# Window attention and a SwiGLU feed-forward on one core: one PSUM pool, RMS chains for pairs of blocks, the attention steps placed by hand, and two more blocks transposed by DMA

## The chip, the cores and the metric

One core of a Trainium2 chip. The metric is the time of one execution of the kernel in microseconds (us), on the device. The profile's span (first to last instruction) is 1.7 to 2.4 us shorter than that time.

Names: PE is TensorE, DVE is VectorE, ACT is ScalarE, POOL is GpSimd, SP is SyncE. "L393" is line 393 of that kernel's source.

## The reference, cut to what matters

```python
def reference(q, k, v, n_sink=4, window=128, w_gate, w_val, w_out, rms_g):
    # q, k, v: 4 batches x 8 heads x 768 positions x 64
    scores = q @ k.T / 8          # kept: the 4 first keys ("sink"), and the last 128 keys
    a = softmax(where(keep, scores, -1e9))
    x = heads side by side (a @ v)               # 3072 tokens x 512
    xn = x / sqrt(mean(x*x) + 1e-6) * rms_g
    g = xn @ w_gate;  val = xn @ w_val           # 512 x 1536 each
    return (g * sigmoid(g) * val) @ w_out        # 1536 x 512
```

## The kernel before

The 3072 tokens are 24 blocks of 128 (six blocks a batch: 0 to 5, 6 to 11, 12 to 17, 18 to 23). Four blocks make a group of the feed-forward part (FFN), so there are six groups, G0 to G5. FFN matmuls of group G are cut into "parts" (four matmuls of 512 columns, 0.86 us of PE by the trace: one part starts at 76.43 us in the kernel before, the next at 77.29), and the attention of later blocks is woven between the parts. A block's "chain" is the row of small DVE instructions that makes 1/sqrt of its mean square (RMS); `xr` is the attention's output times that, and `x(g)` brings it transposed to the FFN as `xnt`. `t(g)` transposes q and k of a block (`qkT`), by a DMA where `by_dma(g)` is true and else on PE (`DMA_T_FROM` is 12, `NT` is 6), `s(g)` makes its scores. `FA` is how many of G0's 12 FFN tiles are done in two halves, first for blocks 0 and 1, later for blocks 2 and 3. PE's and SP's orders are the program's; the order of DVE, ACT and POOL is chosen by the compiler's scheduler, except in the prologue.

```python
def by_dma(g):                      # who transposes q and k of block g: a DMA, or PE
    return g >= DMA_T_FROM and g % NT > 0        # DMA_T_FROM = 12, NT = 6

def unit_sink(b):                   # once a batch: the four sink keys, repacked
    ks = sink.tile([P, HP * KSW], BF16, name="ksk")
    nc.vector.memset(ks, 0.0)
    ksv = ks.rearrange("p (h c) -> p h c", c=KSW)
    for hi in range(2):
        pr = slice(hi * D, (hi + 1) * D)
        nc.vector.tensor_copy(out=ksv[pr, :, hi * NS:(hi + 1) * NS],
                              in_=QKT[b][pr, 1, :, 0:NS])   # keys of the batch's FIRST block
    ...                             # cut

def val():                          # in an FFN part; gate() has made th = tanh(pg / 2)
    pvl = mms("pvl", wv, G, fts, cols)           # a PSUM bank
    nc.vector.scalar_tensor_tensor(out=p1, in0=th, scalar=1.0, in1=pg, ...)   # reads PSUM
    nc.vector.tensor_tensor(out=HT[key], in0=p1, in1=pvl, ...)  # reads PSUM, frees the bank

def step(g):                        # what of the attention goes with block g
    ...                             # cut: sink scores, scores of g, attention of g-1
    if t == 1:
        slots[1].append(lambda: unit_sink(b))    # one step after the batch's first block
    if g + 2 < NB and not by_dma(g + 2):
        slots[2 if t != 5 else 1].append(lambda: unit_t(g + 2))
    if g + 3 < NB and by_dma(g + 3):
        slots[2].append(lambda: unit_t(g + 3))
    ...                             # cut
```

Two things matter later. First, `unit_sink(2)` reads the transposed keys of block 12, and `unit_sink(3)` those of block 18. The condition `g % NT > 0` keeps just these blocks on PE. Second, by the program a PSUM bank that holds `pg` or `pvl` is used again only when DVE has done its product, and the banks are taken in turn.

The softmax here doesn't subtract the row's maximum and nothing guards it: scores larger than these inputs give would overflow.

Of the kernel before, what the change touches and what calls it, by code (L numbers as in the profile page):

```python
# [28 lines left out]
def kernel(  # L29
# [26 lines left out]
    GB = 4  # L56
    NG = NB // GB
    GN = GB * P
# [8 lines left out]

    DMA_X_FROM = 8
    FA = 10
    WEAVE_FROM = 9  # L70
    POOL_MASK_FROM = 2
# [4 lines left out]
    ld = ctx.enter_context(tc.tile_pool(name="ld", bufs=3 * NT))  # L76
# [10 lines left out]
    pools = ExitStack()  # L87
    pp = [pools.enter_context(
        tc.tile_pool(name="psum0", bufs=2, space=bass.MemoryType.PSUM)
    )]  # L90
    PROLOGUE = [True]
    WARM = (3, 4, 5, 2)
# [6 lines left out]
    gb = const.tile([P, DM], FP32, name="gb")  # L99

# [21 lines left out]
    def load_v(g):  # L122
        b, t = divmod(g, NT)
        nc.gpsimd.dma_start(  # L124
            out=V16[b][:, t, :, 0:D],
            in_=v[b, :, t * P:(t + 1) * P, :].rearrange("h t d -> t h d"),
        )

# [30 lines left out]
    raw = [opool.tile([P, DM], FP32, name="osb") for _ in range(3)]  # L159
    for i, src in enumerate((q, k)):  # L160
# [4 lines left out]
    nc.sync.dma_start(  # L165
        out=raw[2][0:1, :], in_=moe_rms_g.rearrange("(o d) -> o d", o=1),
    )
    nc.vector.memset(gb[0:1, 0:P], 1.0)

# [4 lines left out]

    def unit_gb():
        ps = pp[0].tile([P, 512], FP32, name="pgb", tag="ph", bufs=6)
        nc.tensor.matmul(
            out=ps, lhsT=gb[0:1, 0:P], rhs=raw[2][0:1, :], start=True, stop=True,
        )
        nc.scalar.copy(out=gb, in_=ps)  # L180

    with tc.manual_schedule(engines={mybir.EngineType.Pool, mybir.EngineType.DVE}):
# [16 lines left out]
        unit_cast(1)  # L199
        load_k(1)  # L200
# [21 lines left out]
        for g in range(GB + 1, 2 * GB):  # L222
            load_q(g)
            load_k(g)
            load_v(g)
        load_wo(0)
        last_load = load_wo(1)
    with tc.issue_after(last_load):
        for g in range(2 * GB, NB):
            load_q(g)  # L230
            load_k(g)
            load_v(g)


# [9 lines left out]
    def unit_t1(g, i):  # L244

        b, t = divmod(g, NT)
        if t == 0 and i == 0:
            QKT[b] = qkt.tile([P, 2, HP, S], BF16, name="qkT")
        kind = dict(tag="ph", bufs=6) if PROLOGUE[0] and g == 2 else dict(tag="b1")
        ps = pp[0].tile([P, 512], FP32, name="pqk", **kind).bitcast(BF16)  # L250
        transposes(ps, (QS, KS_)[i].pop(g), 0)
        (nc.scalar.copy if g != 1 and i == 0 else nc.vector.tensor_copy)(
            out=QKT[b][:, i, :, t * P:(t + 1) * P],
            in_=ps[:, 0:HP * P].rearrange("p (x c) -> p x c", c=P),
        )

    def by_dma(g):
        return g >= DMA_T_FROM and g % NT > 0

    def unit_t(g):  # L260
# [10 lines left out]
        ps = pp[0].tile([P, 512], FP32, name="pqk", tag="b1").bitcast(BF16)  # L271
# [7 lines left out]
    def unit_sink(b):  # L279
# [11 lines left out]
        for half in range(2):  # L291
            ps = pp[0].tile([P, 512], FP32, name="pvs", tag="b1")
# [14 lines left out]
    def unit_sink_scores(b, t):  # L307

        w = 2 * P
        ps = pp[0].tile([P, 512], FP32, name="pss", tag="b1")  # L310
# [12 lines left out]
    def unit_warm(n):  # L323

        ps = pp[0].tile([P, 512], FP32, name="pw", tag="ph", bufs=6)
# [4 lines left out]

    PTS = {}

    def unit_bias(g, n):

        if PROLOGUE[0]:
            banks = [pp[0].tile([P, 512], FP32, name="ph", tag="ph", bufs=6)
                     for hi in range(2)]
        else:
            banks = [bank() for hi in range(2)]
# [31 lines left out]
    def bank():  # L371
        return pp[0].tile([P, 512], FP32, name="pT", tag="b1")

    def mask(ev, b, t, nq):
        x = ev.shape[1]
        if b < POOL_MASK_FROM or t == 0:
# [16 lines left out]
    def unit_s(g):  # L393
# [17 lines left out]
        for u in range(nb):  # L411
            et = epool.tile([P, 2, per, nq, P], BF16, name="et")
            for hi in range(2):
# [4 lines left out]
                if nq == 1:  # L418
                    mask(et[:, hi], b, t, nq)
            if nq == 2:  # L420
                mask(et.rearrange("p i j n c -> p (i j) n c"), b, t, nq)
            for j in range(per):
                for hi in range(2):
                    for n in range(nq):
                        E[(g, 2 * (u * per + j) + hi, n)] = et[:, hi, j, n, :]

    def halves(g):

        return [slice(0, DM // 2), slice(DM // 2, DM)] if g == 1 else [slice(0, DM)]
# [3 lines left out]
    def unit_sink_av(g):  # L433
        b, t = divmod(g, NT)
        for u in range(2):
            PVB[(g, u)] = pp[0].tile([P, 512], FP32, name="pv", tag="b1")
# [8 lines left out]
    def unit_av(g, u):  # L445
        b, t = divmod(g, NT)

        pv = PVB.pop((g, u)) if t >= 2 else pp[0].tile(
# [12 lines left out]
        if u == 0:  # L461
            X16[g] = xpool.tile([P, H, D], BF16, name="x16")
# [3 lines left out]
        else:  # L466
            unit_norm(g, u, pvv)
            unit_sq(g, u)
        if u == 1 and g >= 2:
            unit_rms(g)  # L470
# [19 lines left out]
    def unit_sq(g, u):  # L490
        if u == 0:
            MS[g] = small.tile([P, 2], FP32, name="ms")
# [4 lines left out]
            accum_out=MS[g][:, u:u + 1],  # L497
        )

    def unit_rms(g):  # L500
        x16 = X16.pop(g).rearrange("p h d -> p (h d)")
        ms = MS.pop(g)
        m = small.tile([P, 1], FP32, name="m")
        nc.vector.scalar_tensor_tensor(
            out=m, in0=ms[:, 0:1], scalar=RMS_EPS, in1=ms[:, 1:2],
# [3 lines left out]
        y = small.tile([P, 5], FP32, name="y")  # L509
        nc.vector.tensor_scalar(  # L510
            out=y[:, 0:1].bitcast(I32), in0=m.bitcast(I32), scalar1=-0.5,
            scalar2=float(0x5f3759df - 2 ** 31), op0=ALU.mult, op1=ALU.add,
        )
        nc.vector.scalar_tensor_tensor(
            out=y[:, 1:2], in0=y[:, 0:1], scalar=y[:, 0:1], in1=m,
            op0=ALU.mult, op1=ALU.mult,
        )
        nc.vector.scalar_tensor_tensor(
            out=y[:, 2:3], in0=y[:, 1:2], scalar=RSQRT_B, in1=y[:, 1:2],
# [3 lines left out]
            out=y[:, 3:4], in0=y[:, 1:2], scalar=RSQRT_A, in1=y[:, 0:1],  # L523
# [3 lines left out]
            out=y[:, 4:5], in0=y[:, 2:3], scalar=RSQRT_C, in1=y[:, 3:4],  # L527
            op0=ALU.add, op1=ALU.mult,
        )
        Y[g] = y  # L530
        X16[g] = x16
        if g >= 2:
            unit_xr(g)

    Y = {}

    def unit_xr(g):
        y, x16 = Y.pop(g), X16.pop(g)
        XR[g] = []
        for c in halves(g):  # L540
            XR[g].append(xpool.tile([P, c.stop - c.start], BF16, name="xr", bufs=3))
            nc.vector.scalar_tensor_tensor(  # L542
                out=XR[g][-1], in0=x16[:, c], scalar=y[:, 4:5], in1=gb[:, c],
                op0=ALU.mult, op1=ALU.mult,
            )
        if g >= DMA_X_FROM:
            G, tb = divmod(g, GB)
            if tb == 0:
                XNT[G] = xtpool.tile([P, KTN, GN], BF16, name="xnt")
            nc.sync.dma_start_transpose(  # L550
                out=XNT[G][:, :, tb * P:(tb + 1) * P], in_=XR.pop(g)[0],
            )

    def unit_x(g):
# [3 lines left out]
        if tb == 0:  # L558
            XNT[G] = xtpool.tile([P, KTN, GN], BF16, name="xnt")
        for xr, c in zip(XR.pop(g), halves(g)):  # L560
            n = c.stop - c.start
            ps = pp[0].tile([P, 512], FP32, name="pxt", tag="b1").bitcast(BF16)
            for i in range(n // P):
                nc.tensor.transpose(
                    out=ps[:, i * P:(i + 1) * P], in_=xr[:, i * P:(i + 1) * P],
                    identity=ident,
                )
            nc.scalar.copy(  # L568
                out=XNT[G][:, c.start // P:c.stop // P, tb * P:(tb + 1) * P],
                in_=ps[:, 0:n].rearrange("p (k c) -> p k c", c=P),  # L570
            )
# [4 lines left out]
    def mms(name, w_sb, G, fts, cols):  # L576

        ps = pp[0].tile([P, 512], FP32, name=name, tag="b1")
# [37 lines left out]
    def parts_o(G, tb):  # L616
        st = {}

        def part(i):
            if i == 0:  # L620
                st["po"] = pp[0].tile([P, 512], FP32, name="po", tag="b1")
# [15 lines left out]
    def step(g):  # L637


        b, t = divmod(g, NT)  # L640
        slots = [[], [], [], []]
# [6 lines left out]
        if g <= NB:  # L648
            if (g - 1) % NT >= 2:
                slots[0].append(lambda: unit_sink_av(g - 1))  # L650
            slots[0].append(lambda: unit_av(g - 1, 0))
            slots[0].append(lambda: unit_av(g - 1, 1))
        if GB <= g - 3 < NB:
            slots[1].append(lambda: unit_x(g - 3))
        if g + 2 < NB and not by_dma(g + 2):
            slots[2 if t != 5 else 1].append(lambda: unit_t(g + 2))
        if g + 3 < NB and by_dma(g + 3):
            slots[2].append(lambda: unit_t(g + 3))
        return slots

    def weave(parts, slots, upto=0, first=False):

        n, i = len(parts) - upto, 0
        for s, f in enumerate(parts):
            if first:
                f()
            while i < len(slots) and i < (s + 1) * len(slots) / n:
                for u in slots[i]:
                    u()
                i += 1  # L670
            if not first:
                f()

    with tc.manual_schedule(engines=MANUAL_ALL):
        unit_warm(6)
# [6 lines left out]
        unit_bias(1, 0)  # L682
        unit_sp(0, 1)
        unit_t1(1, 1)
# [7 lines left out]
        unit_warm(WARM[0])  # L692
        for u in range(2):
            unit_av(1, u)
            unit_norm(1, u, PV[(1, u)])
            unit_sq(1, u)
        unit_gb()
        unit_rms(0)
        unit_xr(0)
        unit_rms(1)  # L700
        unit_xr(1)
        unit_warm(WARM[1])
        unit_x(0)
        unit_t1(2, 0)
        unit_warm(WARM[2])
        unit_x(1)
# [4 lines left out]
        pools.close()  # L711
        pp[0] = ctx.enter_context(
            tc.tile_pool(name="psum", bufs=8, space=bass.MemoryType.PSUM)
        )
        PROLOGUE[0] = False

    with tc.manual_schedule(engines=MANUAL):

# [7 lines left out]
        weave(fa, [  # L726
# [64 lines left out]
```

## Time and profile before

255.18 us, median of three runs (254.96 to 256.45).

The page of the kernel before: busy time by engine, then the busy tenths of PE and the granted clock in 40 slices of 6.4 us.

```profile
PE 240.8 (95%) x1784; PEld 125.2 (49%) x1784; DVE 175.7 (69%) x465; ACT 141.9 (56%) x320; POOL 94.8 (37%) x127
...
PE   6988899989979999999999999999999999999994
...
PEclk9979999999999999999999999999999999999999
```

PE is nearly always busy, so what can be won is time in which PE waits or runs at a lower clock, and work that is taken from it. Note the 7 in the third slice of the clock.

To see how much that is I set the columns of all matmuls (512 columns in 213 ns, the trace's own spacing; the two fp32 ones counted double, which is an estimate: the trace of before has 1.06 us for both of them together, 0.53 us each; warm-up matmuls left out) against the time, stage by stage; a stage ends where the next group's first gate matmul starts. "Lost" is time less work. Small negative values come from rounding the spacing.

| stage | before: time | work | lost | after: time | work | lost |
|---|---|---|---|---|---|---|
| prologue | 19.4 | 5.6 | 13.8 | 16.2 | 4.9 | 11.2 |
| G0 | 57.0 | 51.7 | 5.3 | 55.5 | 47.2 | 8.3 |
| G1 | 36.6 | 36.7 | -0.2 | 48.8 | 40.6 | 8.2 |
| G2 | 37.2 | 37.2 | 0.0 | 38.9 | 36.7 | 2.2 |
| G3 | 36.6 | 37.1 | -0.5 | 38.8 | 37.1 | 1.7 |
| G4 | 32.9 | 32.4 | 0.5 | 33.3 | 32.4 | 0.9 |
| G5 and tail | 34.9 | 30.7 | 4.2 | 35.1 | 30.7 | 4.4 |

The end of the prologue before, in order of time (start, duration, engine, line, operation, out<-in; in brackets the idle time ahead of it and what ended it). PE only:

```profile
15.68 0.63 PE L239 MATMUL pqk<-ident,qs 128*128 128x128 bf16 x4
16.10 2.34 PE L327 MATMUL pw<-idle 128*128 128x512 bf16 x5
18.23 0.63 PE L564 MATMUL pxt<-ident,xr 128*128 128x128 bf16 x4
19.39 0.38 PE L582 MATMUL pg<-xnt,wg 128*128 128x256 bf16 x2 [0.52 <-DMA ks<-in_k_dram]
```

Five idle (warm-up) matmuls take 2.34 us, 427 ns apart, twice the 213 ns, and the granted clock is 0.50 from 15.3 to 18.7 us; the transposes of block 1 stand behind them. The first gate matmul is at 19.4.

What DVE waited for, before (sum, times, longest, us), and what the tile `ksk`, the sink keys, waited for in the same kernel:

```profile
DVE p L600 <- ACT th L595: 18.9, 28, 10.3
DVE rden L480 <- PE pv L457: 10.0, 7, 4.3
DVE m L504 <- ACT sq L495: 9.0, 12, 1.6
```

```profile
its engine sat idle before it (us, times) until:
  issue: 3.0, 8
  PE pss L312: 0.4, 1
  ACT qkT L274: 0.2, 1
```

DVE never waits for a DMA in the main part; the copies of the sink keys wait 0.2 us at most for their keys.

### The profile page before, as it was taken

How to read it: one execution, taken by the hardware profiler on the slowest of the kernel's cores; microseconds unless marked ns; L12 is line 12 of the kernel's file. 1: busy time of each engine (PE TensorE's matmuls, PEld its weight loads, DVE VectorE, ACT ScalarE, POOL GpSimd, SP SyncE). 2: the span in 40 equal slices, each digit the busy share in tenths (PEclk: the TensorE clock that was granted, in tenths of full speed). 3: DMA queues.
4: the chain of work that ended last, by engine and by line, in shares of the span. 5: the costliest groups of instructions: out<-in, count | busy, mean ns of one | idle time of the engine just before them, and what ended most of it. 6: DMA issues, size and time to landing. Idle time of an engine off the chain costs nothing.

```text
span 254.6 us, 4880 instructions
## 1 busy us (share of the span) xinstructions
PE 240.8 (95%) x1784; PEld 125.2 (49%) x1784; DVE 175.7 (69%) x465; ACT 141.9 (56%) x320; POOL 94.8 (37%) x127
## 2 busy tenths in 40 slices
PE   6988899989979999999999999999999999999994
PEld 2536677755534444454454444444444444444441
DVE  4563897998768999348898277998268991277800
ACT  2646678879994565475475366566445341333211
POOL 8986778299987440331231003033121000000000
PEclk9979999999999999999999999999999999999999
DMA  9999999999999999435005328215321101200022
GB/s 130 142 171 190 188 157 189 183 156 155 185 174 168 156 155 118 97 89 147 10 12 64 82 62 147 41 23 64 104 61 45 21 18 63 107 0 0 3 82 82
DMA packets 105849, 25.74 MB, mean 101 GB/s; under 512 B 95073, under 2 KB 102753, under 8 KB 105826
## 3 DMA queue, kind: packets, MB, share of 16 engines
q0 software_dynamic: 80704, 13.90, 70.6%
q1 hardware_dynamic: 24082, 11.28, 20.0%
q10 hardware_dynamic: 1040, 0.26, 0.5%
q8 instruction: 14, 0.23, 0.4%
q14 instruction: 9, 0.07, 0.1%
HBM read 28.31 MB, written 6.29 MB: 136 GB/s over the span
## 4 chain that ended last, share of the span: by engine, by line
PE 68%; DVE 12%; ACT 8%; POOL 4%; DMA 3%; issue 2%; POOLq 0%; DVEq 0%; ACTq 0%
PE po L623 20%; PE pg L582 20%; PE pvl L582 19%; DVE hT L608 3%; DVE p L600 3%; DMA ks<-in_k_dram 3%; PE pT L405 2%; ACT et L414 2%; DVE et L380 2%; ACT sq L495 2%; PE pv L453 2%; PE pv L457 2%; ACT qkT L274 1%; DVE x L485 1%; POOL qs L111 1%
## 5 line engine op out<-in xcount | busy, mean ns | idle before, releaser
L582 PE MATMUL pg<-xnt,wg 128*128 128x512 bf16 (+1 forms) x328 | 74.0, 353 | 2.3 <-ACT xnt L568 1.8
L582 PE MATMUL pvl<-xnt,wv 128*128 128x512 bf16 (+1 forms) x328 | 74.0, 353 | 0.0
L595 ACT ACTIVATE th<-pg 128x512 bf16<-128x512 f32 x72 | 43.2, 600 | 51.2 <-PE pg L582 49.8
L623 PE MATMUL po<-wo,hT 128*128 128x512 bf16 x288 | 64.9, 379 | 0.1
L600 DVE SCALAR_TENSOR_TENSOR p<-th,pg 128x512 bf16<-128x512 bf16 x72 | 49.2, 683 | 18.9 <-ACT th L595 18.9
L608 DVE TENSOR_TENSOR hT<-p,pvl 128x512 bf16<-128x512 bf16 x72 | 49.4, 686 | 5.7 <-PE pvl L582 0.9
L582 PEld LDWEIGHTS <-wg 128*128 128x128 bf16 x328 | 31.4, 98 | 30.9 <-issue 2.7
L582 PEld LDWEIGHTS <-wv 128*128 128x128 bf16 x328 | 31.2, 98 | 28.8 <-issue 0.2
L414 ACT ACTIVATE et<-pT 128x512 bf16<-128x512 f32 x76 | 39.5, 605 | 6.7 <-PE pT L405 6.7
L623 PEld LDWEIGHTS <-hT 128*128 128x128 bf16 x288 | 27.4, 98 | 30.6 <-issue 0.2
L382 POOL TENSOR_SCALAR_AFFINE_SELECT et<-et 128x512 bf16<-128x512 bf16 x20 | 12.6, 637 | 79.7 <-ACT et L414 73.2
L630 ACT ACTIVATE osb<-po 128x512 f32<-128x512 f32 x24 | 14.4, 601 | 27.8 <-PE po L623 25.4
L495 ACT ACTIVATE sq<-x 128x256 bf16<-128x256 bf16 x48 | 20.2, 425 | 7.5 <-DVE x L485 7.1
L111 POOL DMA_DIRECT2D qs<-in_q_dram x23 | 20.9, 907 | 7.0 <-DMA wo<-in_moe_w_out_dram 2.5
L111 POOL DMA_DIRECT2D ks<-in_k_dram x23 | 20.8, 904 | 6.6 <-DMA wo<-in_moe_w_out_dram 2.9
L124 POOL DMA_DIRECT2D v<-in_v_dram x24 | 21.7, 903 | 4.3 <-DMA qs<-in_q_dram 2.7
L485 DVE TENSOR_TENSOR x<-pv,rden 128x256 bf16<-128x256 f32 x48 | 20.0, 422 | 0.9
L380 DVE TENSOR_TENSOR et<-et,masks 128x1024 bf16<-128x1024 bf16 (+1 forms) x22 | 13.9, 636 | 8.5 <-ACT et L414 8.4
L542 DVE SCALAR_TENSOR_TENSOR xr<-x,y,gb 128x512 bf16<-128x512 bf16 (+1 forms) x25 | 18.1, 728 | 0.7
L480 DVE RECIPROCAL rden<-pv 128x4 f32<-128x4 f32 x48 | 7.8, 173 | 10.1 <-PE pv L457 10.0
L405 PE MATMUL pT<-qkT 64*128 64x256 bf16 (+1 forms) x168 | 12.0, 261 | 2.1 <-ACT qkT L274 1.4
L457 PE MATMUL pv<-v,et 128*128 128x65 bf16 x168 | 12.6, 194 | 0.0
(72 smaller groups left out, 198.3 us busy)
## 6 DMA issues: line engine op xcount, KB each, us to landing
out_dram<-osb SPq DMA_DIRECT2D x24, 256.0 KB, 2.2
v<-in_v_dram POOLq DMA_DIRECT2D x24, 128.0 KB, 7.6
qs<-in_q_dram POOLq DMA_DIRECT2D x23, 128.0 KB, 7.5
ks<-in_k_dram POOLq DMA_DIRECT2D x23, 128.0 KB, 7.5
wg<-in_moe_w_gate_dram POOLq DMA_DIRECT2D x6, 256.0 KB, 8.6
wv<-in_moe_w_val_dram POOLq DMA_DIRECT2D x6, 256.0 KB, 8.9
wo<-in_moe_w_out_dram POOLq DMA_DIRECT2D x2, 768.0 KB, 10.7
osb<-in_k_dram ACTq DMA_DIRECT2D x1, 256.0 KB, 4.5
```

What stands on the lines that cost most here:

```text
L111: nc.gpsimd.dma_start(out=tl, in_=src[b, :, t * P:(t + 1) * P, :].rearrange("h t d -> t h d"),)
L124: nc.gpsimd.dma_start(out=V16[b][:, t, :, 0:D], in_=v[b, :, t * P:(t + 1) * P, :].rearrange("h t d -> t h d"),)
L380: nc.vector.tensor_tensor(out=e, in0=e, in1=mv, op=ALU.mult)
L414: nc.scalar.activation(out=et[:, hi].rearrange("p j n c -> p (j n c)"), in_=banks[u][hi], func=ACT.Exp, scale=inv_sqrt_d,)
L485: nc.vector.tensor_tensor(out=X16[g][:, heads_of(g, u), :], in0=pvv[:, :, 0:D], in1=RDEN.pop((g, u)).unsqueeze(2).to_broadcast((P, 4, D)), ...
L495: nc.scalar.activation(out=sq, in_=xh, func=ACT.Square, scale=MS_SCALE, accum_out=MS[g][:, u:u + 1],)
L542: nc.vector.scalar_tensor_tensor(out=XR[g][-1], in0=x16[:, c], scalar=y[:, 4:5], in1=gb[:, c], op0=ALU.mult, op1=ALU.mult,)
L582: nc.tensor.matmul(out=ps[:, i * n:(i + 1) * n], lhsT=w_sb[:, kt, ft * P:(ft + 1) * P], rhs=XNT[G][:, kt, cols], start=(kt == 0), stop=(kt ...
L595: nc.scalar.activation(out=st["th"], in_=st["pg"], func=ACT.Tanh, scale=0.5)
L600: nc.vector.scalar_tensor_tensor(out=p1, in0=st["th"], scalar=1.0, in1=st["pg"], op0=ALU.add, op1=ALU.mult,)
L608: nc.vector.tensor_tensor(out=HT[key][:, i:i + n, cols], in0=p1.rearrange("p (n c) -> p n c", n=n), in1=pvl.rearrange("p (n c) -> p n c", ...
L623: nc.tensor.matmul(out=st["po"], lhsT=HT[(G, ft // 2)][:, ft % 2, tb * P:(tb + 1) * P], rhs=wo[:, ft, :], start=(ft == 0), stop=(ft == FTN ...
```

## The change

Its intent, as its text shows: shorten the prologue (one RMS chain for blocks 0 and 1, the RMS weight multiplied in while their transposes are copied out of PSUM, more warm-up matmuls), use one PSUM pool of eight banks throughout, halve the number of small RMS instructions on DVE by doing two blocks in one chain, put DVE's masks and chains some parts later (`later`), give every attention unit a part number by hand, and take the transposes of blocks 12 and 18 from PE too. The core of the diff:

```diff
-    FA = 10
+    FA = 8                                   # FFN tiles of G0 that are done in two halves
 ...
     def by_dma(g):
-        return g >= DMA_T_FROM and g % NT > 0
+        return g >= DMA_T_FROM
 ...
-        if u == 1 and g >= 2:
-            unit_rms(g)
+        if u == 1 and g >= 2 and g % 2 == 1:
+            later(0 if g < GB else 1 if g < 2 * GB else 3, lambda: unit_rms(g))
 ...                                          # cut: unit_rms works on [P, 2] instead of [P, 1]
+        for i in range(2):
+            later(0 if g < GB else 1 if g < 2 * GB else 1 + i, lambda i=i: unit_xr(g - 1 + i, y[:, 5, i:i + 1]))
 ...                                          # cut: unit_x multiplies by gt at evacuation, ACT and DVE share it
-        if g + 3 < NB and by_dma(g + 3):
-            slots[2].append(lambda: unit_t(g + 3))
+            slots[2].append(lambda: unit_t(g + 2))
+        if g + 4 < NB and by_dma(g + 4):
+            slots[2].append(lambda: unit_t(g + 4))
 ...
-        unit_warm(6)
+        unit_warm(9)
 ...                                          # cut: prologue order; 28 warm-ups instead of 18
+        run(fb[:8], [
+            (0, lambda: unit_bias(3, 1)),
+            (0, lambda: unit_sp(3, 1)),
+            (0, lambda: unit_x(2)),
+            (0, lambda: unit_x(3)),
 ...                                          # cut: part numbers of all other units of G0
+                for g in range(8 if G == 1 else 4 * G + 6, min(4 * G + 10, NB + 1)):
+                    p = 6 * (g - 8) if G == 1 else 9 * (g - 4 * G - 6)
+                    slots += step(g, p, 1.5 if G == 1 else 2)
```

## The prediction

> **What bounds the kernel now.** TensorE. The share table has PE busy 95%, and the windows view has it at 10.0 of 10 us from 80 us on at full clock. All matmuls' columns at the trace's own rate (512 in about 213 ns) make 231 us without the 18 warm-ups; the span is 254.6. So 24 us are lost:
> - Prologue: the first gate matmul starts at 19.4 us (timeline), after about 5 us of real matmul work: 14.5 lost.
> - 19 to 80 us: about 5 us net, in gaps between matmul starts: 0.9 at 22.7 (ACT qkT copy), 0.9 at 26.7 (DVE qkT copy), 0.7 at 37 (xnt of blocks 2, 3), 0.7 at 49, 1.1 at 53 (qkT), 0.5 at 65, 1.7 at 74.6 (xnt of block 7, right before the next group's gate).
> - Tail: about 4 us of last eviction and store.
>
> **What the change does.**
> 1. Prologue. Before, the block-1 RMS chain starts only at 15.14, behind xr(0), which waited for the copy of gb (0.57 us on ACT); its xr takes two STT pieces of 0.48 us on DVE; then its transposes wait behind five warm-up matmuls that ran at clock 0.5 (15.3 to 18.7, windows view: 427 ns each), start at 18.23, and the two ACT copies end at 19.34. After: one chain for both blocks from about 14.0, seven small ops, about 1.2 us; xr(0) as tensor_scalar on DVE at about 0.3 us (the same kind on 512 bf16 elements, the mask conversion, took 0.29; the STT takes 0.75), xr(1) at once on ACT, about 0.6; evictions split over ACT and DVE, 1 to 1.2 us for both. First gate at about 17.2: 2.2 us earlier. [...] 28 warm-ups instead of 18, 12 in that gap, should keep the clock whole.
> 2. Blocks 12 and 18 are transposed by DMA: 16 matmuls of 128 columns fewer, about 0.85 us of PE, where PE is the bound: all gained.
> 3. Placement by hand in parts (masks, squares and chains put off, x(6), x(7) a part earlier): of the 4.5 us lost between 40 and 80 I expect 2 to 3 back. But pairing means that x(2), x(3) wait for block 3's chain right before the second half of group 0: norms, squares, 1.2 us chain, evictions with gt (four small ACT muls or one 0.7 us DVE op), against 4 us of PE work in between: a wait of 1 to 2 us near 30 us. It eats much of the 2.5 us saved in that stage.
> 4. 12 pair chains for 24 save about 10 us of DVE, off the critical path.
>
> **Sum:** -2.2 - 0.85 - 2.4 = about -5.5 us: 249.7.
>
> **Prediction:** 249.7 us, 247.0 to 252.8 in 8 of 10. Chances: faster by over 2% 0.53, within 2% 0.44, slower 0.03.
>
> **What would show it:** first pg at 17 to 17.5; clock 1.0 between 15 and 19; one wait of 1 to 2 us for xnt of blocks 2 and 3; none over 0.5 us at the turn from group 0 to 1; PE gapless after 80; 16 fewer PE transposes.
>
> **What would make it wrong:** the 12 warm-ups running at half clock and pushing x(0) back; the gt load of 4-byte pieces holding up others; DVE near full (about 85% by my count) while group 1 carries five blocks' attention, so that PSUM banks come free late; DMA transposes of the x blocks landing late for group 2.

-2.2, -0.85 and -2.4 come to -5.45, so the 249.7 us can be followed as they stand. That 12 warm-ups in the wait for the RMS chain ("that gap") would keep the clock whole was the author's estimate, not shown by the trace of before; in the kernel after they ran from 11.50 to 14.25 us, and the granted clock was 1.00 from 15 to 19 us. That the load of `gt` could hold up others was a guess, which no run shows (in the kernel after it landed 6.0 us after its issue).

## The result

268.49 us (268.15 to 268.92, four runs) against 255.69 us of the kernel before in the same comparison: ratio 1.0501, 95% interval 1.046 to 1.0542. Slower by 5%. (A ratio is the mean time of one kernel's fast runs over that of the other's of the same rounds, so it is not quite the ratio of the medians.)

The page after, the same lines:

```profile
PE 243.8 (91%) x1760; PEld 123.5 (46%) x1760; DVE 165.7 (62%) x406; ACT 140.3 (53%) x321; POOL 95.2 (36%) x128
...
PE   8989599879964999999999999998899999999994
...
PEclk9999979999995999999999999999999999999998
```

DVE has 10 us less work, as intended, and PE idles more. Two slices of the clock now stand out: the sixth, and the thirteenth with a 5.

The prologue after, as above:

```profile
14.31 0.72 ACT L557 ACTIVATE xr<-x,y 128x512 bf16<-128x512 bf16 x1 [1.28 <-DVE y L546]
14.31 0.54 DVE L559 TENSOR_SCALAR xr<-x,y 128x512 bf16<-128x512 bf16 x1
14.91 0.62 PE L586 MATMUL pxt<-ident,xr 128*128 128x128 bf16 x8 [0.66 <-DVE xr L559]
15.23 1.14 ACT L602 ACTIVATE xnt<-pxt,gt 128x128 bf16<-128x128 bf16 x4 [0.20 <-PE pxt L586]
15.34 0.76 DVE L595 TENSOR_TENSOR xnt<-pxt,gt 128x256 bf16<-128x256 bf16 x2 [0.49 <-PE pxt L586]
...
16.16 1.07 PE L613 MATMUL pg<-xnt,wg 128*128 128x256 bf16 x7 [0.19 <-ACT xnt L602]
```

This part does what was intended: the gate starts at 16.2. What DVE, then `ksk`, then PE waited for after:

```profile
DVE rden L500 <- PE pv L470: 27.3, 8, 8.1
DVE p L631 <- ACT th L626: 23.8, 27, 9.7
DVE ksk L280 <- DMA qkT<-ks: 9.6, 2, 7.1
```

```profile
its engine sat idle before it (us, times) until:
  DMA qkT<-ks: 9.6, 2
```

```profile
PE pT L418 <- DVE hT L639: 5.8, 1, 5.8
PE pxt L586 <- DVE xr L559: 2.8, 3, 2.0
...
PE po L654 <- DVE hT L639: 2.1, 3, 1.5
PE pv L452 <- DVE hT L639: 1.7, 4, 0.5
```

The largest wait of PE is new: 5.8 us, for DVE. DVE in turn waited for a DMA. DVE in order of time, at that place, and PE from the same place:

```profile
74.52 0.68 DVE L631 SCALAR_TENSOR_TENSOR p<-th,pg 128x512 bf16<-128x512 bf16 x1
82.28 0.50 DVE L280 COPY ksk<-qkT 64x16 bf16<-64x16 bf16 x2 [7.08 <-DMA qkT<-ks]
82.81 0.69 DVE L639 TENSOR_TENSOR hT<-p,pvl 128x512 bf16<-128x512 bf16 x1
```

```profile
77.39 0.39 PE L418 MATMUL pT<-qkT 64*128 64x256 bf16 x4
83.55 0.61 PE L418 MATMUL pT<-qkT 64*128 64x256 bf16 x4 [5.77 <-DVE hT L639]
```

Read it from the top. At 75.2 DVE has finished the product `p`. The next instruction in its queue is the copy of block 12's sink keys, which by the program belongs some 30 parts further on (in e2 below, where it is held back, it runs at 98.3 us). Its keys come from a DMA transpose that was issued at 74.6 and lands at 82.25, 7.7 us later, while loads of later blocks are still running. `hT`, which comes next in that queue and whose `pvl` PE had done by 75.7, starts only after the copy, at 82.81; until then the bank of `pvl` stays taken, and PE, whose next scores want that bank, stops at 77.8. Then the clock: busy time by engine and the granted clock (PEclk) in two stretches, after, and before in the same two stretches of time:

```profile
75.00:83.00 8.00, 2.78 (x16) 1.11 (x15) 0.88 (x4) 2.64 (x5) 4.62 (x6) 0.87 2.04 168
83.00:90.00 7.00, 6.03 (x43) 3.08 (x43) 6.41 (x13) 2.68 (x8) 5.12 (x6) 0.66 2.44 153
```

```profile
75.00:83.00 8.00, 6.57 (x56) 3.38 (x56) 6.06 (x16) 4.50 (x9) 6.56 (x8) 1.00 2.28 165
83.00:90.00 7.00, 7.00 (x42) 3.23 (x39) 6.79 (x20) 3.96 (x10) 2.97 (x4) 1.00 1.78 156
```

The columns are PE, PEld, DVE, ACT, POOL, PEclk, DMA share, GB/s. The clock records of the trace have half clock from 81.0 to 87.8 us. So the stop costs 5.8 us and then PE works at half rate for 4.3 us more, which costs half of that, 2.1 us: together 7.9 of the 8.2 us that G1 lost. All four timed runs of this kernel had a mean clock of 0.978 to 0.98.

### The profile page after: what moved, and what is told of

It reads as the page before. It is cut to its first block, busy times and chain, and to the rows that moved or that the text cites. A ratio compares the mean times of both kernels' runs of the same rounds, so it can differ in the third digit from the quotient of the medians.

```text
span 266.6 us, 4789 instructions
## 1 busy us (share of the span) xinstructions
PE 243.8 (91%) x1760; PEld 123.5 (46%) x1760; DVE 165.7 (62%) x406; ACT 140.3 (53%) x321; POOL 95.2 (36%) x128
## 4 chain that ended last, share of the span: by engine, by line
PE 65%; DVE 20%; ACT 5%; DMA 4%; issue 4%; SPq 0%; DVEq 0%; ACTq 0%
PE po L654 21%; PE pg L613 16%; PE pvl L613 14%; DVE hT L639 6%; DVE p L631 5%; DMA qkT<-ks 4%; PE pT L418 3%; DVE xr L563 3%; PE pv L466 2%; PE pw L322 2%; PE pv L470 2%; ACT et L427 2%; ACT sq L515 2%; PE pqk L235 1%; DVE et L393 1%
## 5 line engine op out<-in xcount | busy, mean ns | idle before, releaser
L613 PE MATMUL pg<-xnt,wg 128*128 128x512 bf16 (+1 forms) x320 | 75.8, 364 | 1.0 <-DVE xnt L595 0.8
L613 PE MATMUL pvl<-xnt,wv 128*128 128x512 bf16 (+1 forms) x320 | 74.6, 360 | 0.0
L613 PEld LDWEIGHTS <-wg 128*128 128x128 bf16 x320 | 30.7, 99 | 30.2 <-issue 1.2
L418 PE MATMUL pT<-qkT 64*128 64x256 bf16 (+1 forms) x168 | 12.6, 265 | 6.8 <-DVE hT L639 5.8
L563 DVE SCALAR_TENSOR_TENSOR xr<-x,y,gb 128x512 bf16<-128x512 bf16 x20 | 14.1, 746 | 0.1
```

Source lines behind the costliest of these rows:

```text
L418: nc.tensor.matmul(out=banks[u][hi][:, j * w:(j + 1) * w], lhsT=QKT[b][pr, 1, hp, t * P:(t + 1) * P], rhs=QKT[b][pr, 0, hp, t * P:t * P + ...
L563: nc.vector.scalar_tensor_tensor(out=xr, in0=x16, scalar=y, in1=gb, op0=ALU.mult, op1=ALU.mult,)
L613: nc.tensor.matmul(out=ps[:, i * n:(i + 1) * n], lhsT=w_sb[:, kt, ft * P:(ft + 1) * P], rhs=XNT[G][:, kt, cols], start=(kt == 0), stop=(kt ...
```

## The experiments

The theory A at this point: the order of DVE's queue, by way of the DMA transpose of blocks 12 and 18, costs some 9 of the 13 us; the rest is smaller waits that the hand placement made. Rivals: B, the one pool and the placement cost nearly all; C, the DMA transpose is simply too late for its own users on PE.

Each comparison had the kernel before beside it; where runs of different comparisons are set against each other, the excess over before in each one's own comparison is the safer measure.

### e1: blocks 12 and 18 back on PE

```diff
     def by_dma(g):
-        return g >= DMA_T_FROM
+        return g >= DMA_T_FROM and g % NT > 0
 ...
-        if t == 0:
+        if b not in QKT:        # block 13 is now asked for before block 12
             QKT[b] = qkt.tile(...)
```

> The changed kernel with one part undone: blocks 12 and 18 (first of batches 2 and 3) are transposed on TensorE again. Theory A (the copy of the sink keys, ksk<-qkT, stands some 25 parts early in VectorE's queue and waits there for the DMA transpose; TensorE then stops for 5.9 us and its clock is halved for 6.8 us): both waits of VectorE (7.1 and 2.5 us) vanish, no half clock near 81 us, 257.5 to 260 us. Rival B (the eight-bank pool and the placement of the attention steps cost the time): less than 3 us back, over 265 us.

Measured: 259.88 us, ratio 1.0171 (1.0142 to 1.0199). The excess over before fell from 12.8 to 4.6 us, so 8.2 us came back (8.6 between the two medians, which are of different comparisons). Of DVE's waits for a DMA only 0.9 us are left, for the first loads of the prologue, and G1 lost -0.2 us by the reckoning of the table (8.2 after). A holds. B falls as the main cause; the 4.6 us that stay are what e4 to e7 take apart.

### e2: the DMA transposes kept, only DVE's order changed

```diff
-            nc.vector.scalar_tensor_tensor(out=p1, ...)
+            LASTP[:] = [nc.vector.scalar_tensor_tensor(out=p1, ...).ins]
 ...
-        for hi in range(2):                    # the copies of unit_sink
-            nc.vector.tensor_copy(...)
+        with (tc.issue_after(LASTP[0]) if b >= 2 else ExitStack()):
+            for hi in range(2):                # queued behind the p1 that stands just before in the program
+                nc.vector.tensor_copy(...)
```

> The changed kernel with the DMA transposes of blocks 12 and 18 kept; only VectorE's order differs: the ksk copies of batches 2 and 3 are queued behind the tanh product that stands just before them in the program. Theory A (order alone): like e1 or up to 1 us better because 16 PE transposes stay away: 257 to 259.5 us. Rival C (the DMA transpose itself comes too late for the scores of block 12): a wait of TensorE for qkT near 95 us and over 263 us.

Measured: 259.83 us, ratio 1.0187 (1.0136 to 1.0238): the same as e1, 0.3 us above the range that I expected. What `ksk` waited for in e2:

```profile
its engine sat idle before it (us, times) until:
  issue: 2.1, 6
  DVE hT L642: 0.8, 2
```

By the medians the transposes of `qkT` land no sooner than in the kernel after (3.0 and 2.5 us from issue to landing, against 2.6 and 2.4 there), and neither DVE nor PE has a DMA transpose among its longest waits: C falls. This is the cleanest of the tests, because the same instructions run on the same engines, and in DVE's compiled order nearly nothing else moves than two copies of some 0.2 us, twice: a few of their neighbours change places.

### e3: this part alone, in the kernel before

```diff
     def by_dma(g):                             # in the kernel before
-        return g >= DMA_T_FROM and g % NT > 0
+        return g >= DMA_T_FROM
```

> The kernel before with this one part of the change alone: blocks 12 and 18 transposed by DMA. Its list of VectorE's instructions has the ksk copy of batch 2 right after block 10's normalisation, about when the transpose is issued. Theory A: VectorE waits several us for the DMA, 257 to 263 us. If the part is harmless by itself: 254 to 255 us (16 fewer transposes).

Measured: 262.49 us, ratio 1.0292 (1.0261 to 1.0323): 7.2 us slower, from one condition. DVE in e3, in order of time:

```profile
73.53 0.42 DVE L485 TENSOR_TENSOR x<-pv,rden 128x256 bf16<-128x256 f32 x1
81.11 0.66 DVE L285 COPY ksk<-qkT 64x16 bf16<-64x16 bf16 x2 [7.16 <-DMA qkT<-ks]
```

The same wait, of the same size, with none of the rest of the change. Its trace also has the half clock (83.0 to 89.8 us; 0.51 over the stretch from 83 to 90). So the part is harmful by itself, and it isn't something that the new pool or placement makes.

### e4: e1 with idle matmuls in the wait near 30 us

```diff
         run(fb[:8], [
             (0, lambda: unit_bias(3, 1)),
             (0, lambda: unit_sp(3, 1)),
+            (0, lambda: unit_warm(10)),
             (0, lambda: unit_x(2)),
```

> e1 and ten idle matmuls of 512 columns (2.1 us) put into the wait for blocks 2 and 3 near 30 us. If the half clock from 33.2 to 36.6 us comes from that idle time, it vanishes, and the run is 1.0 to 1.7 us shorter than e1. If the wait itself is what costs and the clock is not due to it: as e1, or up to 0.5 us longer.

Measured: 258.92 us, ratio 1.0137 (1.0079 to 1.0194); 1.0 us less than e1 by the medians, but the runs lie in two clumps (257.4 and 257.7; 260.1 and 260.4, these with a mean clock of 0.993), so the time alone does not decide it. The profiles do. Two stretches of e1, then of e4, columns as above:

```profile
29.20:32.50 3.30, 0.97 (x16) 0.59 (x15) 2.63 (x10) 1.73 (x5) 2.95 (x4) 1.00 1.64 190
32.50:36.00 3.50, 3.14 (x15) 2.26 (x16) 0.89 (x2) 1.09 (x3) 2.44 (x3) 0.51 2.10 198
```

```profile
30.00:33.20 3.20, 2.42 (x17) 1.11 (x15) 2.53 (x9) 1.77 (x6) 2.84 (x4) 1.00 1.76 184
33.20:36.60 3.40, 3.28 (x32) 2.98 (x33) 1.53 (x4) 0.99 (x2) 2.14 (x4) 1.00 2.12 198
```

In e1 PE is busy for 1 of 3.3 us, and the clock is halved for the next 3.4 us (0.51 over 3.5 us). With idle matmuls PE is busy for 2.4 of 3.2 us and the clock stays at 1.00. G0 lost 6.9 us instead of 8.3. In the two slower runs of e4 the clock fell somewhere that no profile shows.

### e5: e4 with the attention steps of G2 to G4 four parts later

```diff
-                    p = 6 * (g - 8) if G == 1 else 9 * (g - 4 * G - 6)
+                    p = 6 * (g - 8) if G == 1 else 9 * (g - 4 * G - 6) + 4
```

> e4 with the attention steps of groups 2 to 4 four parts later, so that VectorE's RMS chain and its two xr (1.4 us) come behind the last product hT of a group's FFN part and not in front of it. If VectorE's queue being too full there is what TensorE waits for in groups 2 to 4 (1.35, 1.41 and 0.88 us lost in e4), that loss falls to 0.5 us or less in each: 2 to 3 us off e4, 256 to 257 us. Rival (PSUM banks of the one pool taken in another order): no change.

Measured: 255.84 us, ratio 1.0003 (0.9974 to 1.0032); 1.7 us less than the mean of e4's two runs with the higher clock. G2, G3 and G4 lost 0.2, 0.7 and 0.0 us (e4: 1.35, 1.4 and 0.9). DVE at the end of G2's FFN part in e4:

```profile
135.89 1.41 DVE L563 SCALAR_TENSOR_TENSOR xr<-x,y,gb 128x512 bf16<-128x512 bf16 x2
137.22 0.68 DVE L631 SCALAR_TENSOR_TENSOR p<-th,pg 128x512 bf16<-128x512 bf16 x1
137.82 0.34 DVE L280 COPY ksk<-qkT 64x16 bf16<-64x16 bf16 x2
138.19 0.69 DVE L639 TENSOR_TENSOR hT<-p,pvl 128x512 bf16<-128x512 bf16 x1
```

Two blocks' `xr`, 1.41 us, stand ahead of the last products, for which the output matmuls wait (0.63 us up to 138.94). Those `xr` are needed only by a later group. In e5 they come after the last `hT`, in the output parts. So the placement by hand had put this lump into the FFN parts (the third of a group's four steps begins at part 18 of 24 there, and at 22 in e5), where DVE was busy for 20.4 of 25.1 us, and not into the output parts, where it was busy for 4.2 of 13.4 us (both G2 of e4).

### e6: e4 with a chain for each block again

```diff
-        if u == 1 and g >= 2 and g % 2 == 1:
+        if u == 1 and g >= 2:
 ...                                    # unit_rms on [P, 1] for g >= 2, its xr one part later
```

> e4 with an RMS chain for each block from block 2 on, as before the change (12 more small chains, some 10 us more VectorE time). If pairing is what makes TensorE wait (for blocks 2 and 3 at 31 us, blocks 4 and 5 at 57 us, and at the end of the FFN parts): 1.5 to 3 us faster than e4. If VectorE's load is the cause whatever its order: slower than e4 by 1 us or more. Neither: within 0.7 us.

Measured: 257.27 us, ratio 1.0056 (1.0027 to 1.0084), against e4's 1.0137. G2 and G3 lost 0.3 and 0.5 us (e4: 1.35 and 1.4), G0 6.4 (6.9); but G1 lost 0.5 (-0.2) and G4 1.2 (0.9). So with eleven more chains, that is, more DVE work, PE waited less at the ends of G2 and G3. How much that brings in all, the times leave open: 1.7 us by the medians, but only 0.3 us against e4's two runs with the higher clock (257.4 and 257.7), and all runs of e6 had a clock of 1.0. It seems an overlapping cure with e5: in both the lump is gone from the end of the FFN parts.

### e7: e4 with FA = 10

```diff
-    FA = 8
+    FA = 10
 ...
-        run(fb[:8], [
+        run(fb[:10], [
-            (0, lambda: unit_warm(10)),
+            (0, lambda: unit_warm(4)),
 ...                                    # later part numbers of G0 scaled by 15/19
```

> e4 with FA = 10 as before the change: two more parts (1.7 us of matmuls) between the attention of block 3 and the transposes of x(2), x(3), and four idle matmuls there instead of ten. If the wait there is a matter of the work left to cover the chain: the idle time plus warm-ups there (about 3.0 us together in e4) falls by 1.2 to 1.7 us, and group 0 is that much shorter. If VectorE's queue grows with it: as e4.

Measured: 256.86 us, ratio 1.0037 (1.0003 to 1.0071). G0 lost 5.4 instead of 6.9 us, the 1.5 us that two more parts of cover were to bring (0.7 us of it show against e4's two runs with the higher clock). The wait for blocks 2 and 3 is thus a matter of work left to cover the chain; some of the gain was given back in a 2.0 us wait for a `qkT` copy at 50 us (1.2 in e4), since the scaled part numbers had moved two units together.

### e8: the kernel before with other warm-ups

```diff
-    WARM = (3, 4, 5, 2)
+    WARM = (3, 9, 1, 2)
```

> The kernel before, with nine instead of four warm-up matmuls ahead of x(0) and one instead of five ahead of x(1). If its prologue lost 2 to 3 us to the half clock and to warm-ups in the way, the first gate comes at 16.5 to 17.5 instead of 19.4 us; if the later stages wait for loads anyway, half of that is given back: 253.5 to 254.8 us. If the prologue of before does not suffer on average: 255 to 255.6.

Measured: 255.69 us, ratio 0.9994 (0.9966 to 1.0023); the first gate at 18.4, not 16.5 to 17.5. A miss. Two things came out of it. The trace gives full clock only from 8.7 us on, so where the clock first rises seems to count, and not the later warm-ups alone. And the profile of before that I had read was of one sort of run: 256.35 us at a mean clock of 0.993, while 13 of the 14 runs of before in the first two comparisons had 0.997 or more (in the last two, 14 of 22). The prologue of before stands unchanged in e3 and in e12 too. In e3 the clock was full from 4.5 us on and the first gate came at 16.6; in e12 it was full from 4.0 us on, fell to half from 14.2 to 17.6, and the gate came at 18.0.

### e9 and e10: the repairs together

e9 is e5 with FA = 10, `unit_warm(5)`, `t1(4, 1)` ahead of the wait, and new part numbers in G0 (the core of the diff):

```diff
-            (1, lambda: unit_t(6)),
+            (0, lambda: unit_t(6)),
+            (1, lambda: unit_t(7)),
 ...
-            (3, lambda: unit_t(7)),
-            (5, lambda: unit_s(6)),
+            (4, lambda: unit_s(6)),
 ...                                    # cut: the rest fitted to 16 parts
```

e10 is e9 with blocks 12 and 18 on DMA and the copies held back as in e2.

> The repairs together: e5 (transposes of blocks 12 and 18 on TensorE, attention steps four parts later) with FA = 10, five idle matmuls ahead of x(2), t(7) two parts earlier so that its copy on ScalarE is done before the scores of block 6, and x(4) after five more output parts. If the separate losses add up: e5 less 1.4 (FA) and less 2 of the 3.2 us that e5 loses between 48 and 58 us: 252.5 to 254 us, 0.5 to 1.2% faster than before. If each wait only moves to the next one: 255 to 256.

> e9 with blocks 12 and 18 on the DMA transpose again and the sink copies held back in VectorE's queue as in e2. If the 16 transposes of 128 columns are worth what I predicted once VectorE's order is repaired: 0.5 to 0.9 us faster than e9. If the DMA transposes' traffic or the held-back copies cost as much as they save (e2 was as fast as e1): within 0.4 us of e9.

Measured: e9 254.52 us, ratio 0.9958 (0.9935 to 0.9981); e10 253.13 us, ratio 0.9906 (0.9883 to 0.993). The losses add up roughly, not fully (e9 was expected at 252.5 to 254). With DVE's order repaired, the DMA transposes are worth 1.4 us by the medians, more than the 0.5 to 0.9 that I expected. (The traces of these two and of e11 and e12 lack some matmul records, so I give no losses by stage for them.)

### e12: the part done in order, in the kernel before

The edits of e3 and e2 together, in the kernel before.

> The kernel before with blocks 12 and 18 transposed by DMA as in e3, but the sink copies held back in VectorE's queue as in e2. If the order alone made e3 lose 7 us, and the part is worth the 0.85 us that I had predicted: 254.4 to 255.2 us against before's 255.7, no wait of VectorE for a DMA. If the early DMA transposes hurt the kernel before in another way as well: above 256 us.

Measured: 255.59 us, ratio 0.999 (0.9961 to 1.0019), and no wait of DVE for a DMA after the prologue. The loss of e3 is gone, so order alone made it. The 0.85 us is not there: at most some 0.4% (1 us), within noise. Why the same part brings 1.4 us in e10 and perhaps nothing here, no run tells. The clock may hide some of it: five of e12's six runs had a mean clock of 0.993, and five of the eleven runs of before beside it; among these the means are 255.7 and 256.2 us.

### e11: e10 with a chain for each block

The edit of e6 on e10.

> e10 with one RMS chain for each block from block 2 on. If pairing still costs waits in group 0 and near the ends of groups there: 0.4 to 1.5 us faster than e10 (251.7 to 252.8). If the chains' extra 10 us of VectorE now count, since the queue is nearly full in group 1: 0.5 us or more slower.

Measured: 252.45 us, ratio 0.9867 (0.9839 to 0.9895); 1.3% faster than the kernel before, the best of all here, and correct. By the medians pairing still cost 0.7 us, in an arrangement in which the lump at the end of the groups had already been moved; but e10 and e11 are of different comparisons and their intervals overlap, so this is likely and not shown.

## Why the prediction was wrong

I predicted 249.7 us (247.0 to 252.8) and 3% for slower by over 2%. It was 268.49. The excess over before, each time in its own comparison, goes from 12.8 us (after) to 4.6 (e1: step 1 below undone), 3.6 (e4: idle matmuls) and 0.2 (e5: attention steps later), so even with these three undone nothing of the predicted gain of 5.5 us shows; e9, e10 and e11 are 1.2, 2.6 and 3.4 us below before. By steps:

1. **"Blocks 12 and 18 are transposed by DMA: 16 matmuls of 128 columns fewer, about 0.85 us of PE, where PE is the bound: all gained."** This is the step that failed. I costed what PE no longer does, and did not ask who else reads the result. `unit_sink` reads the keys of just these two blocks on DVE, and the scheduler placed that copy early in DVE's queue, where it had to wait 7.1 us (block 12) and 2.5 us (block 18) for the DMA. Through the PSUM bank of `pvl` PE stopped for 5.8 us and lost some 2 more at half clock. Measured by e1 and e2: plus 8.2 us in place of minus 0.85. The condition that the diff removed, `g % NT > 0`, may have been a sign that somebody had met this before.
2. **Prologue, "first gate at about 17.2: 2.2 us earlier".** The time of the gate was better than predicted (16.2), and the clock was full from 15 to 19 us. But the gain was read off one run, and the gate of before moves: it came at 16.6 (e3), 18.0 (e12), 18.4 (e8, whose warm-ups differ) or 19.4, later where the clock rises late (at 8.5 to 8.7 us instead of 4.0 to 4.5: e8 and before) or falls again (e12 and before). After's was at 16.2, and at 15.7 to 16.7 in e1, e2 and e4 to e7. No run isolates the prologue, so its gain in the timed runs stays open; it lies between nothing and 3 us.
3. **"Of the 4.5 us lost between 40 and 80 I expect 2 to 3 back"; "a wait of 1 to 2 us near 30 us".** The mechanism of the wait near 30 us was right and its size too small: 2.15 us ahead of the transposes and 0.95 us behind them, and then 3.4 us at half clock (0.50 from 33.2 to 36.6), which e4 shows to come from the idle time (1.00 there with idle matmuls in it). The wait at the turn from group 0 to 1 is gone, as predicted. But new waits of 1.2, 1.0 and 1.3 us came at 50, 56 and 58 us (a `qkT` copy, DVE products, `xr` of the pair), so nothing came back: G0 lost 8.3 us where before lost 5.3.
4. **"PE gapless after 80".** Wrong beyond step 1: in G2, G3 and G4 after lost 2.2, 1.7 and 0.9 us, before 0.0, -0.5 and 0.5 (0.6 to 0.8 of G2's 2.2 go with block 18's copy: e1 lost 1.4 there, e2 1.7). I had named the cause among the risks ("DVE near full ... so that PSUM banks come free late"), but for group 1. There it did not happen by itself: with step 1 undone G1 lost nothing (e1). It was the ends of the FFN parts of groups 2 to 4. e5 takes most of it away in all three, e6 in G2 and G3.
5. **"12 pair chains for 24 save about 10 us of DVE, off the critical path."** The 10 us are right (175.7 to 165.7), and so is that they were off the path. I missed that a pair makes the chain later and its two `xr` a lump of 1.4 us, which stands ahead of the last `hT` (e4: `xr` at 135.89, `hT` only at 138.19); with more DVE work e6 lost 1.0 and 0.9 us less in G2 and G3, and e11 is faster than e10 by the medians.

The chances were too sure as well. I gave 3% to slower although I could not see the order in which the scheduler would put DVE's instructions, and the change touched that order everywhere.

On the clock and on the order of DVE's queue the traces show this. Two have half clock after a stretch in which PE mostly idled: for 3.4 us after PE had been busy for 1 of 3.3 us (e1), and for 6.8 us from 81.0 on, 3.2 us into the 5.8 us stop (after). One does not: in the kernel before, the half clock from 15.3 to 18.7 came after 3.4 us in which PE was busy for 2.7 us, so that stretch was not idle, and what halves the clock in every case is not shown. In DVE's queue the 7.08 us ahead of two copies that took 0.50 us together, with `hT` behind them, is what one early reader costs there.

## What to carry to other kernels

When work moves from an engine to a DMA, look for every reader of the result on every other engine, and for where the compiled program puts that reader in its queue; here the saving on the busiest engine (0.85 us by my estimate) was a tenth of what one early reader cost (8.2 us). If it stands too early, hold it back in its own queue: that was a repair here (the excess over before fell from 12.8 us to 4.5 in e2), and with it the saving showed in e10 (1.4 us) but not in e12. Less work on an engine that isn't the limit gained nothing here (10 us of DVE), and joining two small chains can lose, if what it delays or lumps together stands ahead of products that PE waits for (1.41 us of `xr` ahead of the last `hT` in e4; 1.35 us lost in G2, 0.2 in e5).

## What else the traces show

- The time from issue to landing of a DMA transpose. In the kernel after, the median over `qkT` transposes was 2.4 to 2.6 us, but the four issued between 72 and 77 us, while the loads of 128 KB were running, took 7.6 to 8.7 us (block 12's keys 7.7); the twenty issued from 104 us on, after the last load had landed, took 2.4 to 4.3 us. The median in the profile's list of DMA issues hides this.
- The start of the clock. With one and the same prologue, the first gate came at 16.6 us (e3), 18.0 (e12) and 19.4 (before): 2.8 us apart, 1.1% of the span. The clock was full from 4.5, 4.0 and 8.5 us on, and in the last two it was half again for 3.4 us. So the spread is that of the first rise and the second fall together. How much of it reaches the end was not measured.
- How busy PE was before the clock fell. It fell at 15.3 us in before and at 14.2 in e12, each time after 3.4 us in which PE was busy for 2.7 us; in e3 PE was as busy from 11.3 to 14.7 and the clock stayed full. What decides, no run tells.
